# Transposes of q' in the rounded format, from buffers that DMAs fill, and rest products with 128 rows

## The chip, the cores and the metric

The kernel runs on one core of a Trainium2 chip. The metric is the device time of one execution, in microseconds (us); the median of several runs is given. The core's engines run beside each other: TensorE (PE; PEld are its weight loads), VectorE (DVE), ScalarE (ACT), GpSimd (POOL) and SyncE (SP). SP and POOL also issue the DMAs here.

## The reference

Two mixing blocks are gated together, with S = 2048 rows, D = 576 columns, H = 32 heads of Dh = 18:

```
g = sigmoid((x * gate_w).sum(-1, keepdims=True))
# a: linear attention
q, k, v = heads of x @ wqkv
pq, pk = phi(q), phi(k)          # phi(t) = (t + 1 if t > 0 else exp(t)) + 1e-6
kv = einsum("bhsd,bhse->bhde", pk, v);  z = pk.sum over s
o = (pq @ kv) / (pq @ z + 1e-6)
a = o @ wo
# b: real part of a 2-D DFT of a second input, by matrices
b = Cr @ (xb @ Dr.T) - Ci @ (xb @ Di.T)
out = g * a + (1 - g) * b
```

(In this kernel the second input is the same x.) All data are 32-bit floats.

## The kernel before, in words

**Products in a rounded format.** TensorE multiplies in fp32r (`R` in the code), a rounded 32-bit format. To keep precision, an operand is split in two: ScalarE writes its rounded value (`hi_of`, L196), VectorE writes the rest, `operand - hi` (`lo_of`, L206), and a product is made of three: hi·hi, hi·lo, lo·hi. Plain additions are `add` (L216). `run` (L226) issues a list of products into one of eight PSUM banks.

**The stages.** 576 columns are four chunks of 128 and a rest of 64; 2048 rows are 16 tiles of 128.

1. k' = phi(x wk) for all tiles (L558 and L226), to about 64 us, then the products of x with k' (L725) and with wv (L704, L707, the kv matrices in three PSUM banks), to about 134 us.
2. q' = phi(x wq) for 16 tiles, `q_tile` (L226, tiles `wd`, `xs`): 14 products for each half of 288 columns (290 in the second, which carries the gate). ScalarE (L393, L394) and VectorE (L395) turn each half into `acc[i]`. In between M = kv·wo is built (`build_kv`, `build_m`), moved by GpSimd's DMAs (`move_m`, L886 to L889) and split (`split_m`, tiles `mw`). `normalise(k)` divides the pair of tiles 2k, 2k+1 by the denominators, in four parts on VectorE (L796, L797, L800, L801, L804); for the transposes it copies the last 64 columns of both tiles to `last` (L809).
3. The attention's second product, `q' M`, from about 192 to 258 us, a loop over 16 tiles. `transposed(k)` turns a normalised pair on TensorE with the identity: eight transposes of 128x128 (L826) and one for the two rests (L827), in the full format, straight from `acc` into PSUM; ScalarE and VectorE split the result into `qs`. For each half of a tile 14 products with M follow (`m_steps`). ScalarE scales by the gate (L1239), and GpSimd stores the row to `att` (L1241). The pair k is turned in iteration 2k-1 (pair 0 at the end of stage 2).
4. `Hidden.run`, twice: the DFT along D for seven combinations of blocks (a Strassen-like scheme, `PRODUCTS`), 392 products at L1012. Each product of 576 is 6 products of 128 rows (tiles `xf` or `xb`) and one of 96 rows for the rest (tile `xr`; hi, lo and hi of 32 rows one below the other). `Left` and `right` prepare the combinations of x and of the DFT matrix, in pieces that run between other work: `right`'s third piece (k = 2) makes the rest rows.
5. `sequence`, after each `Hidden.run`: the DFT along S, 1344 products at L1171, whose matrices are combined and split by VectorE and ScalarE as they arrive, and the mixing with the gate (L1188).

**What sets the order.** SyncE, ScalarE and VectorE run in the order of the program's text (`manual_schedule`); ScalarE and VectorE from the first stage on. TensorE does so only from the loop of stage 3 on; before, the framework's scheduler orders it. GpSimd's queue is ordered by that scheduler all along. By hand are set: `early`, which says after which q' tile a part of `norms`, of the third piece or of x's pair 7 (`seven`) is done; `plan`, the same for stage 3; and the tables of iterations at which SyncE issues loads. `begin_after` makes an instruction wait for another one. All buffers lie at fixed addresses of one arena, and later uses of an address wait for earlier ones.

Of the kernel before, what the change touches and what calls it, by code (L numbers as in the profile page):

```python
# [142 lines left out]
def kernel(  # L143
# [111 lines left out]
    ident = const([P, P], F, "ident")  # L255
    make_identity(nc, ident)
# [142 lines left out]
    xrest = scratch([NP * 96, 7 * P], "xr")  # L399
    xrest_of = xrest.rearrange("(g q j r) n -> g j r q n", g=2, q=4, j=3)  # L400
# [54 lines left out]
    def right(src, rest, order):  # L455

        main, last = scratch([P, 7, 2, 2, HALF], "wm"), scratch([96, 7, HALF], "wm")

        def load(k, start):
            c = at(start, [P, 7, 2, HALF], R, "wb")[:P if k < 2 else 96]  # L460
            r, raw = c.bitcast(F)[:, :, 1], src[k] if k < 2 else rest
            for a, b in ((slice(0, 3), slice(0, 3)), (5, 3)):
                begin_after(nc.gpsimd.dma_start(out=r[:, a], in_=raw[:, b]), done[-1])
            return c

        def piece(k, start):

            c = load(k, start)
            r = c.bitcast(F)[:, :, 1]
            yield  # L470
# [4 lines left out]
            add(r[:, 6], r[:, 4], r[:, 1], ALU.subtract)  # L475
            yield
            hi_of(c[:, :, 0], r)
            yield
            if k < 2:
                for fs in (slice(0, 4), slice(4, 7)):  # L480
                    lo_of(c[:, fs, 1], r[:, fs], c[:, fs, 0])
                    nc.gpsimd.dma_start(out=main[:, fs, k], in_=c.bitcast(F)[:, fs])
                    if fs.start == 0:
                        yield
            else:
                rows = slice(32, 64)
                lo_of(c[rows, :, 0], r[rows], c[rows, :, 0])
                yield
                nc.gpsimd.dma_start(out=last, in_=c.bitcast(F)[:, :, 0])

        return (main, last), [piece(*o) for o in order]
# [127 lines left out]
    def xg_next(lo_of=lo_of):  # L619
        if xg_raw:  # L620
# [4 lines left out]
            else:  # L625
# [4 lines left out]
                                              (2, T_AT + 76544)))  # L630
# [145 lines left out]
    def q_tile(i):  # L776
# [14 lines left out]
    def normalise(k):  # L791
# [10 lines left out]
        for i in range(2):  # L802
# [4 lines left out]
            if i == 1:  # L807
                lasts.append(at(last_ring.next(), [P, 2, REST], F, "last"))
                nc.vector.tensor_copy(out=lasts[-1], in_=acc_pairs[k][:, :, KC * P:])  # L809
            yield  # L810

    lasts, last_ring = [], Ring(T_AT + 92672, 2 * REST * 4, 3)
# [5 lines left out]
    def transposed(k):  # L818

        both = [at(qs_ring.next(), [P, 9, P], R, "qs") for _ in range(2)]  # L820
        mains = [bank(), bank()]
        last = bank()[:, :P]
        for i in range(2):
            for c in range(KC):
                cs = slice(c * P, (c + 1) * P)
                nc.tensor.transpose(mains[i][:, cs], acc[2 * k + i][:, cs], ident)  # L826
        nc.tensor.transpose(last, lasts.pop(0).rearrange("p a b -> p (a b)"), ident)  # L827
# [3 lines left out]
        for i, t in enumerate(both):  # L831
            mine, other = ((slice(0, REST), slice(REST, P))[j] for j in (i, 1 - i))
            hi_of(t[mine, 8], last[mine])
            lo_of(t[other, 8], last[mine], t[mine, 8])
        return both
# [56 lines left out]
    def split_m(h):  # L892
        hi_of(mhi[:, :KC, h], mraw[:, :, h])
        lo_of(mlo[:, :, h], mraw[:, :, h], mhi[:, :KC, h])
        hi_of(mhi[:, KC, h], mrest[:, h])
# [15 lines left out]
    for f in wo_split:  # L911
        f()
    kv_step(4)
    q_tile(1)
    build_kv()
# [7 lines left out]
    early = {4: [(norms, 2)], 5: [(norms, 1), (wr_pieces[2], 1)],  # L923
             6: [(norms, 1)], 7: [(wr_pieces[2], 1)],
             8: [(wr_pieces[2], 1), (norms, 1)], 9: [(wr_pieces[2], 1), ("seven", 1)],
             10: [("seven", 1)], 11: [(wr_pieces[2], 1)],
             12: [(wr_pieces[2], 1), ("seven", 1)], 14: [("seven", 1), (norms, 1)],
             15: [("seven", 1), (norms, 1)]}
    for i in range(4, NT):
        for part in early.get(i, ()) if i > 12 else ():  # L930
            go(seven if part[0] == "seven" else part[0], part[1])
        q_tile(i)
# [5 lines left out]
        for part in early.get(i, ()) if i < 13 else ():  # L938
            go(seven if part[0] == "seven" else part[0], part[1])
        if i == NT - 3:  # L940
            queue = transposed(0)
        if i in (10, 11):
            split_m(i - 10)
# [26 lines left out]
    class Hidden:  # L970
# [4 lines left out]
        def load_w(self, k):  # L975
# [5 lines left out]
            nc.sync.dma_start(out=wl.bitcast(F), in_=self.main[:, f].rearrange("p c s n -> p (c s) n"))  # L981
            nc.sync.dma_start(out=rl.bitcast(F)[:96], in_=self.last[:, f])
            self.w[k] = wl, rl

        def load_rest(self, p):

            self.rest[p] = at(self.lay.rest(p), [P, 7, P], R, "xr")
            n = min(NP * 96 - p * 96, P)
            nc.sync.dma_start(out=self.rest[p].bitcast(F)[:n], in_=xrest[p * 96:p * 96 + n])

        def load_x(self, p, k):
# [3 lines left out]
            nc.sync.dma_start(out=t.bitcast(F), in_=xforms[p][:, a:b])  # L995
# [134 lines left out]
    def sequence(m, g, src, dst, last=None, between=None):  # L1130
# [100 lines left out]
    paced.enter_context(tc.manual_schedule(engines={mybir.EngineType.PE}))  # L1231
    for i in range(NT):
# [9 lines left out]
        go(norms, 1 if i in (4, 6) else 2)  # L1242
        for k, n in plan.get(i, ()):
            go(made[k], n)
# [150 lines left out]
```

## Time and profile before

| | |
|---|---|
| median of three runs | 716.61 us (716.57 to 717.23) |
| the profiled execution's own time | 717.38 us |
| its span, first to last instruction | 715.7 us |
| stage 3, from the first m_steps to the first L1012 | about 192.8 to 258.4 us |
| `Hidden.run`, first and second | 51.5 and 52.1 us |
| `sequence`, first and second | 175.2 us each on TensorE |

The page lists busy times, the groups of instructions by line and tile, the chain of work that ended last, and the DMAs. In a group's row stand the line, the engine, the operation, output<-inputs with moving operand first, the shape, the count; then busy time in us and the mean duration of one in ns; then the engine's idle time just before them. In the chain's rows stand start, length and what ran, in us. Durations of matmuls overlap, since they are pipelined: a product that lasts 293 ns holds TensorE for about 130 ns of the chain. A row of a timeline has start and length in us, and a row of the windows has the stretch, its length, and each engine's busy time. A row of DMAs has the count, the size, and the median time from issue to landing.

### The profile page before, as it was taken

Reading aid. Unit: us, or ns where it says so; the run is one execution under the profiler, and the core shown is the slowest. Engines: PE = TensorE matmul, PEld = TensorE weight load, DVE = VectorE, ACT = ScalarE, POOL = GpSimd, SP = SyncE. Lnnn points to the kernel's source line nnn. Section 1 sums busy time; section 2 is a strip of 40 time slices with the busy share of each in tenths; the row PEclk is TensorE's granted clock in tenths of the full one; section 3 lists DMA queues with packets and bytes.
Section 4 is the critical chain, followed back from the end, with each engine's and each line's share of the span. In section 5 each row is a group of like instructions: output and inputs, shape, how many; then the busy total and the mean of one; then the engine's idle time right before and its main releaser. Section 6 shows DMA issues by size and latency. Waiting matters only on the chain.

```text
span 715.7 us, 13965 instructions
## 1 busy us (share of the span) xinstructions
PE 711.6 (99%) x5436; PEld 711.1 (99%) x5436; DVE 601.1 (84%) x1020; ACT 338.5 (47%) x587; POOL 54.9 (8%) x94
## 2 busy tenths in 40 slices
PE   9999999999999999999999999999999999999998
PEld 9999999999999999999999999999999999999998
DVE  5699977687999748989999999857889988888885
ACT  5998445677644444553534334323535433343331
POOL 1112200050131110000010000000000000000000
PEclk9999999999999999999999999999999999999999
DMA  7388896874594589753475675789973544454530
GB/s 259 105 280 312 318 303 209 301 213 129 180 368 183 195 307 366 237 184 118 150 257 184 212 254 208 278 312 402 377 260 94 184 132 144 127 181 155 179 131 34
DMA packets 57525, 157.84 MB, mean 221 GB/s; under 512 B 6388, under 2 KB 15668, under 8 KB 56436
## 3 DMA queue, kind: packets, MB, share of 16 engines
q1 hardware_dynamic: 48404, 118.44, 48.9%
q0 software_dynamic: 8768, 38.12, 14.7%
q8 instruction: 43, 0.70, 0.4%
q10 hardware_dynamic: 288, 0.39, 0.2%
q14 instruction: 22, 0.18, 0.1%
HBM read 114.06 MB, written 41.39 MB: 217 GB/s over the span
## 4 chain that ended last, share of the span: by engine, by line
PE 99%; DVE 0%; issue 0%
PE bank L1171 49%; PE bank L226 23%; PE bank L1012 14%; PE bank L725 8%; PE bank L558 2%; PE bank L826 1%; PE bank L252 1%; PE bank L704 0%; PE bank L707 0%; PE bank L827 0%; DVE row L1188 0%
## 5 line engine op out<-in xcount | busy, mean ns | idle before, releaser
L1171 PE MATMUL bank<-fh,c 128*128 128x288 f32 x1792 | 350.7, 293 | 0.0
L1171 PEld LDWEIGHTS bank<-fh,c 128*128 128x128 f32 x1792 | 285.1, 188 | 0.0
L1171 PE MATMUL bank<-fl,c 128*128 128x288 f32 x896 | 262.3, 293 | 0.0
L196 ACT ACTIVATE c<-craw 128x768 fp32r<-128x768 f32 (+2 forms) x148 | 126.9, 900 | 163.6 <-DVE craw L216 154.0
L1171 PEld LDWEIGHTS bank<-fl,c 128*128 128x128 f32 x896 | 168.2, 188 | 0.0
L206 DVE TENSOR_TENSOR c<-craw,c 128x768 fp32r<-128x768 f32 (+3 forms) x148 | 146.1, 1024 | 0.8 <-ACT c L196 0.8
L226 PE MATMUL bank<-wd,xs 128*128 128x288 f32 (+1 forms) x784 | 104.9, 294 | 0.0
L226 PEld LDWEIGHTS bank<-wd,xs 128*128 128x128 f32 x784 | 103.5, 188 | 0.0
L1012 PE MATMUL bank<-wf,xf 128*128 128x288 f32 x588 | 90.8, 294 | 0.0
L1012 PEld LDWEIGHTS bank<-wf,xf 128*128 128x128 f32 x588 | 83.3, 189 | 0.0
L226 PE MATMUL bank<-mw,qs 128*128 128x288 f32 x448 | 60.7, 295 | 0.0
L725 PE MATMUL bank<-pk,c 128*128 128x288 f32 x448 | 60.0, 294 | 0.0
L725 PEld LDWEIGHTS bank<-pk,c 128*128 128x128 f32 x448 | 59.1, 188 | 0.0
L226 PEld LDWEIGHTS bank<-mw,qs 128*128 128x128 f32 x448 | 59.0, 188 | 0.0
L216 DVE TENSOR_TENSOR craw<-craw,craw 128x256 f32<-128x256 f32 x128 | 54.4, 425 | 5.1
L216 DVE TENSOR_TENSOR ys<-bank,ys 128x288 f32<-128x288 f32 x63 | 28.8, 457 | 28.2 <-PE bank L1171 25.7
L216 DVE TENSOR_TENSOR craw<-craw 128x512 f32<-128x512 f32 x64 | 43.9, 687 | 7.6 <-PE bank L1171 3.7
L196 ACT ACTIVATE fh<-fl 128x864 fp32r<-128x864 f32 (+1 forms) x36 | 30.3, 868 | 28.0 <-DVE fl L216 20.0
L395 DVE SCALAR_TENSOR_TENSOR acc<-bank,e 128x288 f32<-128x288 f32 x64 | 28.6, 454 | 16.5 <-ACT e L394 16.3
L206 DVE TENSOR_TENSOR fl<-fl,fh 128x864 fp32r<-128x864 f32 (+1 forms) x36 | 35.4, 988 | 1.6
L1012 PE MATMUL bank<-wf,xr 96*128 96x288 f32 x112 | 33.3, 298 | 0.0
L216 DVE TENSOR_TENSOR fl<-bank,y 128x288 f32<-128x288 f32 x48 | 21.8, 454 | 11.1 <-PE bank L1012 9.6
(106 smaller groups left out, 662.1 us busy)
## 6 DMA issues: line engine op xcount, KB each, us to landing
xf<-xm SPq DMA_DIRECT2D x42, 512.0 KB, 9.2
craw<-in_cr_dram SPq DMA_DIRECT2D x32, 512.0 KB, 3.9
craw<-in_ci_dram SPq DMA_DIRECT2D x32, 512.0 KB, 3.7
xm<-xb POOLq DMA_DIRECT2D x8, 1024.0 KB, 6.6
wf<-wm SPq DMA_DIRECT2D x14, 576.0 KB, 6.4
xraw<-in_xa_dram SPq DMA_DIRECT2D x25, 320.0 KB, 3.5
xr<-xr SPq DMA_DIRECT2D x14, 448.0 KB, 8.5
xm<-xb POOLq DMA_DIRECT2D x8, 768.0 KB, 8.2
```

The lines of the kernel that those rows point to most:

```text
L196: return nc.scalar.activation(dst, src, AF.Copy, bias=bias)
L206: nc.vector.tensor_tensor(out=dst, in0=src, in1=hi, op=ALU.subtract)
L216: nc.vector.tensor_tensor(out=dst, in0=a, in1=b, op=op)
L226: nc.tensor.matmul(ps, a, b, start=(n == 0), stop=(n == len(pairs) - 1))
L252: nc.tensor.matmul(warm[:, :136], unit[:, :P], unit, start=True, stop=True)
L395: nc.vector.scalar_tensor_tensor(dst, ps, 0.0, e, op0=ALU.max, op1=ALU.add)
L558: nc.tensor.matmul(ps[i][h], x[:, i_x * P:(i_x + 1) * P], wkt.row(h, j), start=(c == 0 and n == 0), stop=(c == KC and n == 1))
L725: nc.tensor.matmul(ps[h][:, :HALF], t[:, a, k], pk[s][:, b, half(h)], start=(s == 0 and n == 0), stop=(s == NT - 1 and n == len(turn) - 1))
L826: nc.tensor.transpose(mains[i][:, cs], acc[2 * k + i][:, cs], ident)
L1012: nc.tensor.matmul(ps, a, b, start=(start and n == 0), stop=(n == len(ops) - 1), skip_group_check=True)
L1171: nc.tensor.matmul(ps[q], c[x][l > 2][:, l - 3 * (l > 2), k], factors[p](y, f), start=(p == 0 and i == 0), stop=(p == NP - 1 and i == 2))
```

## The change

- The identity is made in the full format, then rounded by ScalarE into an `R` tile. `transposed` becomes a generator `turn`, whose 9 transposes have `R` input, identity and output.
- VectorE's copy to `last` goes. When a pair is normalised it is put on a list; `move_normal`, called at the end of each q' tile and of each iteration of stage 3, has GpSimd issue two DMAs for it: 4 x 128 columns of both tiles, and the 64 left of both, into buffers (`turn_at`) of type `R`. The transposes read these.
- TensorE runs in the text's order from `build_kv()` on. In `q_tile` the halves are mixed: 9 products of half 0, 9 of half 1, 5 of half 0, 5 of half 1. The transposes of pair 0 stand in the middle of q' tile 13.
- `split_m` becomes `m_hi` (after q' tiles 9 and 10) and `m_lo` (10 and 11).
- `early` and `plan` are rearranged; two more parts of `norms` are done before stage 3, and the parts of pairs 4 to 7 come one iteration earlier.
- The rest products of `Hidden` take 128 rows: the fourth 32 rows of the weights are zeros, the rows of x are whatever follows. The rest piece (`rest_piece`) works on 64 partitions with half the columns each, and stores eight blocks of 32 rows; x's rest tensor gets 32 rows of zeros at its end.
- The loads of x's pair 2 are spread over iterations 4, 6, 8 and 10, and these and the weights' loads wait for the ScalarE instruction that came last (`begin_after`). Near the end of the first `sequence` one rest load is issued later.

The diff, cut to its core:

```diff
-    ident = const([P, P], F, "ident")
-    make_identity(nc, ident)
+    unit_f = at(SLOT_AT + P * 4, [P, P], F, "unit_f")
+    make_identity(nc, unit_f)
+    ident = const([P, P], R, "ident")
+    nc.scalar.activation(ident, unit_f, AF.Copy)
...
+        def rest_piece(start):
+            c = at(start, [2 * 32, 3, 7, HALF // 2], R, "wb")
+            f = c.bitcast(F)
+            r = f[:, 1]
+            load(r, rest)
+            nc.gpsimd.memset(f[:, 2], 0.0)
+            yield
+            for _ in sums(r):
+                pass
+            yield
+            hi_of(c[:, 0], r)
+            yield
+            lo_of(c[:, 1], r, c[:, 0])
+            for k, a in enumerate((0, 1, 0, 2)):
+                for q in range(2):
+                    ps, cs = slice(q * 32, q * 32 + 32), slice(q * HALF // 2, (q + 1) * HALF // 2)
+                    nc.gpsimd.dma_start(out=last[k * 32:k * 32 + 32, :, cs], in_=f[ps, a])
+            if src is wr:
+                nc.gpsimd.dma_start(out=xrest[NP * 96:], in_=f[:32, 2].rearrange(
+                    "p f n -> p (f n)")[:, :7 * P])
...
-        for h in range(2):
-            ps = bank()[:, :QH[h]]
-            run(ps, steps(xs, lambda j: wqt.row(h, j)))
+        both = [bank()[:, :QH[h]] for h in range(2)]
+        todo = [list(steps(xs, lambda j, h=h: wqt.row(h, j))) for h in range(2)]
+        for part in (slice(0, 9), slice(9, 14)):
+            for h in range(2):
+                for n in range(part.start, part.stop):
+                    nc.tensor.matmul(both[h], *todo[h][n], start=(n == 0), stop=(n == 13))
+            if part.start == 0:
+                next(between, None)
...
-                lasts.append(at(last_ring.next(), [P, 2, REST], F, "last"))
-                nc.vector.tensor_copy(out=lasts[-1], in_=acc_pairs[k][:, :, KC * P:])
+                normal.append(k)
...
+    def move_normal():
+        while normal:
+            k = normal.pop(0)
+            main = at(turn_at[k], [P, 2, KC * P], R, "turn")
+            last = at(turn_at[k] + 2 * KC * P * 4, [P, 2, REST], R, "turn")
+            for t, cs in ((main, slice(0, KC * P)), (last, slice(KC * P, D))):
+                nc.gpsimd.dma_start(out=t.bitcast(F), in_=acc_pairs[k][:, :, cs])
+            moved.append((main, last))
...
-                nc.tensor.transpose(mains[i][:, cs], acc[2 * k + i][:, cs], ident)
-        nc.tensor.transpose(last, lasts.pop(0).rearrange("p a b -> p (a b)"), ident)
+                nc.tensor.transpose(mains[i][:, cs].bitcast(R), main[:, i, cs], ident)
+        nc.tensor.transpose(last.bitcast(R), rest.rearrange("p a b -> p (a b)"), ident)
+        yield
...
+    paced.enter_context(tc.manual_schedule(engines={mybir.EngineType.PE}))
     build_kv()
...
-    early = {4: [(norms, 2)], 5: [(norms, 1), (wr_pieces[2], 1)],
-             6: [(norms, 1)], 7: [(wr_pieces[2], 1)],
-             8: [(wr_pieces[2], 1), (norms, 1)], 9: [(wr_pieces[2], 1), ("seven", 1)],
-             10: [("seven", 1)], 11: [(wr_pieces[2], 1)],
-             12: [(wr_pieces[2], 1), ("seven", 1)], 14: [("seven", 1), (norms, 1)],
-             15: [("seven", 1), (norms, 1)]}
+    early = {4: [(norms, 2), (wr_pieces[2], 1)], 5: [(norms, 1)],
+             6: [(norms, 2), (wr_pieces[2], 1)], 7: [(wr_pieces[2], 1), (norms, 1)],
+             8: [(wr_pieces[2], 1), (norms, 1)], 9: [("seven", 1), (norms, 1)],
+             10: [("seven", 1), (norms, 1)], 12: [("seven", 1)], 14: [("seven", 1)],
+             15: [("seven", 1)]}
...
-            nc.sync.dma_start(out=rl.bitcast(F)[:96], in_=self.last[:, f])
+            if after is not None:
+                begin_after(move, after)
+            nc.sync.dma_start(out=rl.bitcast(F), in_=self.last[:, f])
...
-            ops.append((self.rest[p][:96, 6 - k], wl[:96]))
+            ops.append((self.rest[p][:, 6 - k], wl))
...
-        3: [(0, 1)], 4: [(0, 1)], 5: [(0, 1)], 6: [(0, 1)], 7: [(0, 1)],
-        11: [(1, 1)], 12: [(1, 1)], 13: [(1, 1)], 14: [(1, 2)],
+        2: [(0, 1)], 3: [(0, 1)], 5: [(0, 1)], 10: [(0, 1)], 11: [(0, 1), (1, 1)],
+        12: [(1, 1)], 13: [(1, 1)], 14: [(1, 2)],
...
-        go(norms, 1 if i in (4, 6) else 2)
+        go(norms, 1 if i in (3, 5) else 2)
         for k, n in plan.get(i, ()):
             go(made[k], n)
+        move_normal()
...
-        for k, j in enumerate((9, 10, 12, 4, 5, 6, 14)):
+        for k, j in enumerate((9, 10, 12, 3, 5, 7, 14)):
             if i == j:
-                hidden.load_w(k)
+                hidden.load_w(k, done[-1])
...
-        if i == 3:
-            hidden.load_pair(2)
+        for k, j in ((0, 4), (2, 6), (4, 8), (6, 10)):
+            if i == j:
+                hidden.load_x(2, k, done[-1])
```

More of the change, by code (lines that the diff above doesn't have):

```diff
@@ L475, in piece @@
             add(r[:, 6], r[:, 4], r[:, 1], ALU.subtract)
+        def piece(k, start):
+            c = at(start, [P, 7, 2, HALF], R, "wb")
+            r = c.bitcast(F)[:, :, 1]
+            load(r, src[k])
+            yield
+            yield from sums(r)
             yield
@@ L834, in transposed @@
             lo_of(t[other, 8], last[mine], t[mine, 8])
+    def transposed(k):
+        both = []
+        for _ in turn(k, both):
+            pass
         return both
@@ L931 @@
             go(seven if part[0] == "seven" else part[0], part[1])
-        q_tile(i)
+        if i == NT - 3:
+            queue = []
+            turning = turn(0, queue)
+            q_tile(i, turning)
+        else:
+            q_tile(i)
         build_m({4: (2, 3), 5: (4,)}.get(i, ()))
```

81 lines of the change are left out of this document (40 added, 41 removed).

## The prediction

> **What bounds the kernel now.** I read the page's busy shares and clock first, then the chain that ended last, then the groups by line and shape, and last the stretch from 134 to 258 us by windows and by timeline, since the diff edits little else.
>
> ```profile
> span 715.7 us, 13965 instructions
> PE 711.6 (99%) x5436; PEld 711.1 (99%) x5436; DVE 601.1 (84%) x1020; ACT 338.5 (47%) x587; POOL 54.9 (8%) x94
> PEclk9999999999999999999999999999999999999999
> PE 99%; DVE 0%; issue 0%
> ```
>
> TensorE is busy 711.6 of 715.7 us, at the full granted clock in every slice, and the chain that ended last is 99% TensorE. No wait is there to be removed. The time can fall only if some of the 5,436 matmuls become shorter, and it can rise if one of them has to wait. So I price each edit on TensorE, then ask which new wait could open a hole. The chain, in order of time, prices instructions in their place:
>
> ```profile
> 82.82 0.12 PE bank L704
> 82.94 0.06 PE bank L707
> 83.00 0.17 PE bank L704
> 83.17 0.06 PE bank L707
> ...
> 196.50 0.87 PE bank L826 x8
> 197.38 0.11 PE bank L827
> 197.49 7.29 PE bank L226 x56
> ...
> 258.40 51.52 PE bank L1012 x392
> 309.92 175.21 PE bank L1171 x1344
> 485.13 52.09 PE bank L1012 x392
> ```
>
> A pair of q' tiles costs 0.87 + 0.11 = 0.98 us for its nine transposes (L826, L827), that is 0.109 us each, and then 56 products with M. There are eight pairs, so all transposes hold TensorE for 7.8 us.
>
> **The transposes in the rounded format.** The count stays at 72, with data and identity in fp32r. No transpose of this kind is in the trace, so I look at neighbours.
>
> ```profile
> L826 PE MATMUL bank<-ident,acc 128*128 128x128 f32 x64 | 8.4, 272 | 0.0
> L826 PEld LDWEIGHTS bank<-ident,acc 128*128 128x128 f32 x64 | 7.5, 140 | 0.0
> L707 PE MATMUL bank<-gt,plain 128*126 128x126 f32 x20 | 4.4, 222 | 0.0
> L707 PE MATMUL bank<-gt,plain 128*72 128x72 f32 x5 | 1.0, 201 | 0.0
> L707 PEld LDWEIGHTS bank<-gt,plain 128*126 128x126 f32 x20 | 3.8, 189 | 0.0
> L707 PEld LDWEIGHTS bank<-gt,plain 128*72 128x72 f32 x5 | 0.7, 144 | 0.0
> ```
>
> L707 is a rounded matmul of 126 columns: 222 ns, and 0.06 us on the chain. From 72 to 126 columns the duration grows by 21 ns over 54 columns, 0.39 ns a column. The full-format transpose of 128 columns lasts 272 ns, 50 ns more than L707, which is just another 128 columns at 0.39 ns: its moving side looks like two passes, and a rounded one should need one. That gives 0.06 us a transpose.
>
> The weight load could spoil this. L704 after L707 costs 0.17 us instead of 0.12: a short matmul leaves the next load 0.05 us uncovered, and a pair of loads takes 0.17 + 0.06 = 0.23 us, 0.115 each. But transposes load in 140 ns, as long as an ordinary load of 72 columns, against 189 ns for 126. So a transpose's load looks short already, and I assume that this is a property of transposing and stays. The sum per pair: 9 x 0.06 + 0.05 for the first product after them, whose ordinary load is then uncovered, = 0.59 us against 0.98. That is 0.39 us less, times 8 = **3.1 us gained**. The bounds are 3.6 us (no uncovered load: 9 x 0.05 x 8) and -0.4 us (each held to 0.115: 9 x 0.115 = 1.035, 0.05 more per pair). I take 3.1, as the 140 ns row is the nearest.
>
> The Trainium skill speaks against it: by "TensorE: Matmul & The Clock Gate", section "LDWEIGHTS (loading the stationary operand)", a load takes its columns divided by 1.2 GHz, and its table of weight-path modes gives 32-bit formats no fast load. My estimate from that is 107 ns for any 128 columns, so transposes would stay at 0.107 us and gain nothing. The trace agrees for L707's pairs (0.115) but not for the transposes' 140 ns.
>
> **Rest products with 128 rows.**
>
> ```profile
> L1012 PE MATMUL bank<-wf,xf 128*128 128x288 f32 x588 | 90.8, 294 | 0.0
> L1012 PE MATMUL bank<-wf,xr 96*128 96x288 f32 x112 | 33.3, 298 | 0.0
> ```
>
> The 96-row products last 298 ns and their 128-row neighbours 294: 112 x 4 ns = **0.45 us gained**. Above, it can't exceed what the stage loses against L1171: 51.52/392 = 131.4 ns a product (132.9 in the second stage) against 175.21/1344 = 130.4, so 0.4 + 1.0 = 1.4 us. Below it is nothing, if the 4 ns belong to closing a group and not to the rows. The same section of the Trainium skill says that a load's time doesn't depend on rows; by that alone this term is nothing. The weights' added quarter is zeros.
>
> **TensorE in the text's order, halves mixed 9-9-5-5, high parts of M first.** The same 28 matmuls run per q' tile.
>
> ```profile
> 134.52 48.59 PE bank L226 x366
> ```
> ```profile
> L394 ACT ACTIVATE e<-e 128x288 f32<-128x288 f32 x64 | 28.5, 445 | 2.0
> L393 ACT ACTIVATE e<-bank 128x288 f32<-128x288 f32 x64 | 25.6, 399 | 11.2 <-PE bank L226 7.6 <-PE bank L558 3.6
> ```
> ```profile
> 158.96 0.59 POOL L889 DMA_DIRECT2D mw<-mf  x1 [1.32 <-issue]
> ```
> ```profile
> 175.11 1.48 ACT L196 ACTIVATE mw<-mw 128x1152 fp32r<-128x1152 f32 x2
> ```
>
> The chain has no hole here that a better order could close; at most the 48.59/366 = 132.8 ns a product would fall to the 130.4 of L1171, 0.9 us. A loss comes if an evacuation is late, now that the two halves of a tile end close together: 0.40 + 0.45 = 0.85 us of ScalarE, once. I cost it at nothing, as two banks per tile are held and eight exist. M's first half is split one tile (28 x 0.133 = 3.7 us) earlier than at 175.1, at 171.4; its last move was issued at 159.0, 12 us ahead.
>
> **The copies to the turn buffers.** This is the new wait. After normalising a pair, GpSimd issues two DMAs (512 and 64 KB), and the transposes of that pair wait for them; behind the waiting transposes stand all of TensorE's later matmuls. The copy of columns on VectorE (L809) goes.
>
> ```profile
> 242.33 1.43 DVE L804 SCALAR_TENSOR_TENSOR acc<-acc,den 128x576 f32<-128x576 f32 x2
> 243.79 0.23 DVE L809 COPY last<-acc 128x128 f32<-128x128 f32 x1
> ```
> ```profile
> 238.08 0.87 PE bank L826 x8
> 238.95 0.11 PE bank L827
> 239.06 7.34 PE bank L226 x56
> 246.40 0.87 PE bank L826 x8
> ```
> ```profile
> att<-acc POOLq DMA_DIRECT2D x10, 288.0 KB, 3.4
> xm<-xb POOLq DMA_DIRECT2D x1, 1024.0 KB, 5.9
> ```
> ```profile
> L1241 POOL DMA_DIRECT2D att<-acc x16 | 8.8, 547 | 47.9 <-ACT acc L1239 47.8
> L888 POOL DMA_DIRECT2D mw<-mf x1 | 0.6, 612 | 0.0
> ```
>
> The last pair is the tightest. It is normalised by 243.8 and turned at 246.4: 2.6 us. The change puts two more parts of the normalising into the q' stage, so pairs 4 to 7 finish one tile earlier, in iterations 4, 6, 8 and 10 for use in 7, 9, 11 and 13. A pair with its transposes takes 246.40 - 238.08 = 8.32 us, a tile half of it, 4.2 us. The cover is 2.6 + 4.2 = 6.8 us, less some 0.4 because TensorE is faster: 6.4 us. The need is two issues of about 0.6 us and a landing of 3.4 to 5.9 us (576 KB lies between those sizes): 4.6 to 7.1, middle 5.8. So I cost the copies at **nothing**, with 0.6 us of cover left in the middle case and up to 0.7 us missing at each of four pairs in the worst one of this stretch.
>
> VectorE must keep pace with a faster TensorE as well:
>
> ```profile
> 226.00:234.40 8.40, 7.80 (x15) 1.00 0.62 249
> 234.40:242.70 8.30, 7.27 (x14) 1.00 0.58 182
> ```
>
> It works 7.3 to 7.8 us of each 8.3 us pair (second number). A pair would take 7.9 us; VectorE loses 0.23 us of L809 per pair and two parts of 0.75 to 1.5 us altogether to the q' stage, where the rest piece shrinks by about as much (half as many columns per instruction, 64 partitions). It just fits.
>
> **What is moved on the queues.** SyncE's weight loads and the loads of x's pair 2 now wait for a ScalarE instruction of their iteration. Queued behind them are only loads for the stage at 258.4; the latest, of iterations 14 and 15, stand where they stood, so nothing. GpSimd gets eight stores instead of one for each rest piece, a small memset and the store of zeros: with 0.6 us each some 6 us, in the q' stage, on an engine busy 8% of the span. What stands behind them are copies needed tiles later. The identity's rounding on ScalarE lies at the start, long before its use.
>
> **The sum.** The profiled run took 717.38 us, 1.7 us outside its span and 0.8 above the median of 716.61. 717.38 - 3.1 - 0.45 = 713.8 for such a run; the median falls by the same 3.6, to **713.0**. About 0.2%, 1.4 us, is what a measurement of this kernel can tell from no change.
>
> **The rivals.** *The transpose keeps its pace* (chance 0.20). Either the load holds it to 0.115 us or transposing takes two passes in both formats. For it: the ordinary loads' 0.115, and that a rounded transpose isn't in the trace; against it: the 140 ns. Time: between 716.61 + 0.4 - 0.45 = 716.6 and, with 0.109 kept, 716.2. No measurable change.
>
> *The copies come late* (0.14), the case on the other side. Place: the transposes of pairs 4 to 7. It decides when issue and landing exceed 6.4 us. A store of xm ahead of the copy on GpSimd's queue, which waits for VectorE, or a landing as at the end of the q' stage would do it:
>
> ```profile
> xm<-xb POOLq DMA_DIRECT2D x1, 1024.0 KB, 9.9
> ```
>
> With that landing, 1.2 + 9.9 - 6.4 = 4.7 us are missing at a pair. With half of it, 2.3 us, at four pairs: 9 us lost against 3.6 won, 722. It outweighs the gain from 0.9 us a pair, and shows as slower from 1.25. Against it: the change spreads the loads that fill the DMA queues in that time.
>
> *VectorE paces the pairs* (0.06): with 7.8 us and the 0.3 us that it waits for ScalarE in each pair, it allows 8.1 instead of 7.9, and half of the gain stays: 714.8.
>
> **How the numbers follow.** Forecast 0.60, rivals 0.20, 0.14, 0.06. Faster by over 0.2% (below 715.2): 0.60 + 0.06 less a little for small stalls, 0.64. Same: 0.20 + 0.02 = 0.22. Slower: 0.14. The low end takes half of what the three upper bounds lie above the values taken (0.5 transposes, 0.95 rest, 0.9 order): 713.0 - 1.2 = 711.8. The high end takes in the first rival with 0.115 (716.6) and half of the order's loss and of its missing rest term: 717.2. The forecast's own range is 711.8 to 714.8.
>
> **What would show it.** Right: L826 at about 222 ns and 0.06 us on the chain, the first product after them about 0.05 longer, pairs every 7.9 us, L1012's rest group at 294 ns, no idle on TensorE. Wrong: transposes still at 0.11 us on the chain with equal durations (first rival), or idle before L826 put down to DMA turn (second), or to VectorE before L226 (third).

## The result, and the profile after

The changed kernel takes 723.67 us (median of six runs, 721.50 to 724.95); the kernel before, on the same chip, 717.14 us (716.57 to 717.75). The ratio is 1.0087, with an interval of 1.0075 to 1.0099: slower by 6.5 us, where 3.6 us of gain were forecast. The profiled execution took 722.13 us, 1.5 below its median, and its span grew by 4.7 us; so the profile shows somewhat less than the whole loss.

The page of the kernel after: span, busy time, share of the chain that ended last.

```profile
span 720.4 us, 14032 instructions
PE 711.4 (99%) x5436; PEld 710.6 (99%) x5436; DVE 595.4 (83%) x1012; ACT 336.4 (47%) x588; POOL 76.7 (11%) x127
PE 93%; DMA 3%; issue 2%; POOL 1%; DVE 0%; ACT 0%; POOLq 0%; SPq 0%
```

TensorE's busy time hardly changed, yet the span is 4.7 us longer, and the chain, 99% TensorE before, now has links through DMAs and GpSimd. Its waits, by line, in us in total, number, longest:

```profile
PE bank L1069 <- DMA wf<-wm: 2.4, 1, 2.4
PE bank L863 <- DMA turn<-acc: 1.8, 1, 1.8
...
PE bank L864 <- DMA turn<-acc: 0.7, 1, 0.7
```

L863 and L864 are the transposes, which wait for the new copies; L1069 is the product of the hidden stage (L1012 before), which waits for its weights: it is the seventh product of x pair 0. What the change was priced to shorten, on the chain and in the groups:

```profile
196.16 0.64 PE bank L863 x8
196.80 0.09 PE bank L864
196.89 7.42 PE bank L226 x56
204.31 0.64 PE bank L863 x8
204.95 0.08 PE bank L864
205.03 7.37 PE bank L226 x56
212.41 0.02 issue
```
```profile
L863 PE MATMUL bank<-ident,turn 128*128 128x128 f32 x64 | 6.5, 245 | 1.8 <-DMA turn<-acc 1.8
...
L863 PEld LDWEIGHTS bank<-ident,turn 128*128 128x128 f32 x64 | 6.2, 140 | 2.0 <-DMA turn<-acc 2.0
...
L1069 PE MATMUL bank<-wf,xr 128*128 128x288 f32 x112 | 33.2, 297 | 0.0
```
```profile
490.24 51.72 PE bank L1069 x392
```

A pair's nine transposes take 0.73 us in place of 0.98. A pair with its 56 products takes (212.41 - 196.16)/2 = 8.12 us in place of 8.32, 1.6 us over eight pairs. The second hidden stage takes 51.72 in place of 52.09 us. Both gains are there. (The mean of 297 ns for the rest products takes in some that ran at half the clock, see below.) What eats them is on the chain of waits, in order of time:

```profile
222.08 8.31 DMA turn<-acc
230.39 0.04 issue
230.43 0.87 PE bank L863 x8
...
253.14 3.49 DMA att<-acc
...
256.77 10.60 DMA wf<-wm
267.37 0.14 issue
267.51 47.52 PE bank L1069 x350
```

The copy of pair 5 lands 8.31 us after its issue, and TensorE starts at once when it is there: the copy was what it waited for. The last weights need 10.60 us, after they have waited for a store of the attention rows (`att`), whose buffer they take. The last two loads of weights issue at 255.07 and 256.77 us, close together; in the kernel before they issue at 246.73 and 254.50. Windows of the span show why: stretch, length, busy time of PE, PEld, DVE, ACT, POOL, granted clock, share of the DMA engines, GB/s. First the kernel before, then after:

```profile
217.00:221.00 4.00, 4.00 (x33) 4.00 (x31) 3.88 (x7) 3.07 (x5) 0.56 (x1) 1.00 0.19 74
221.00:231.00 10.00, 10.00 (x82) 10.00 (x81) 9.16 (x16) 4.66 (x11) 1.92 (x4) 1.00 0.65 236
...
241.00:254.00 13.00, 13.00 (x103) 13.00 (x102) 6.54 (x15) 6.86 (x14) 1.62 (x3) 1.00 0.59 191
```
```profile
217.00:221.00 4.00, 4.00 (x35) 4.00 (x35) 2.44 (x5) 3.01 (x6) 0.67 (x2) 1.00 0.97 312
221.00:231.00 10.00, 8.18 (x67) 7.95 (x65) 6.97 (x12) 3.47 (x9) 3.43 (x6) 1.00 1.02 358
...
241.00:254.00 13.00, 12.28 (x98) 12.16 (x97) 5.46 (x13) 5.93 (x13) 3.70 (x7) 1.00 0.97 360
```

In each of these stretches the DMA engines went from partly idle (0.19, 0.65, 0.59) to full. And the copies don't leave GpSimd when a pair is ready. From the timeline of GpSimd (start, length, line, what, idle before):

```profile
213.24 0.57 POOL L1297 DMA_DIRECT2D att<-acc  x1 [1.48 <-ACT acc L1295]
215.04 0.70 POOL L847 DMA_DIRECT2D turn<-acc  x1 [1.22 <-DVE qs L206]
216.37 0.72 POOL L847 DMA_DIRECT2D turn<-acc  x1 [0.63 <-issue]
...
221.38 0.57 POOL L1297 DMA_DIRECT2D att<-acc  x1 [3.00 <-ACT acc L1295]
222.08 1.45 POOL L847 DMA_DIRECT2D turn<-acc  x2
```

| pair | normalised | first copy issued | copies landed | transposes waited |
|---|---|---|---|---|
| 4 | 210.68 | 215.04 | 220.03, 220.43 | no |
| 5 | 219.54 | 222.08 | 230.39, 230.60 | 1.82 us |
| 6 | 229.14 | 230.72 | 237.48, 237.65 | no |
| 7 | 239.18 | 240.49 | 245.42, 248.12 | 0.72 us |

Each first copy issues 1.3 to 4.4 us after its pair is ready: it stands behind the `att` store of the iteration, which waits for ScalarE. Ahead of the copies of pairs 4 and 6 GpSimd then stands idle for another 1.2 and 0.6 us; the last section comes back to that.

After the longest idle time TensorE runs at half its clock. The third-last column is the granted clock:

```profile
267.51:271.14 3.63, 3.63 (x16) 3.63 (x17) 1.64 (x3) 0.10 (x1) 0.00 (x0) 0.53 1.03 421
```

The sixteen products from 267.51 take 3.7 us; at 0.131 each they would take 2.1, so 1.6 us are lost. The account of the span: -1.6 (transposes), +1.8 and +0.7 (pairs 5 and 7), +0.2 (the transposes behind the wait, 0.87 in place of 0.64), which is +1.1; then the first hidden stage, which starts 1.2 us later than before (259.47 against 258.24) and ends 5.1 us later (315.03 against 309.92): +3.9, which is +2.4 for the wait for weights and +1.6 for the clock, less some 0.1 gained; and -0.4 in the second hidden stage. That is +4.6 of the 4.7 us.

### The profile page after: what moved, and what is told of

The parts are those of the page before. It is cut to its first block, busy times and chain, and to the rows that moved or that the text cites. A ratio compares the mean times of both kernels' runs of the same rounds, so it can differ in the third digit from the quotient of the medians.

```text
span 720.4 us, 14032 instructions
## 1 busy us (share of the span) xinstructions
PE 711.4 (99%) x5436; PEld 710.6 (99%) x5436; DVE 595.4 (83%) x1012; ACT 336.4 (47%) x588; POOL 76.7 (11%) x127
## 4 chain that ended last, share of the span: by engine, by line
PE 93%; DMA 3%; issue 2%; POOL 1%; DVE 0%; ACT 0%; POOLq 0%; SPq 0%
PE bank L1228 49%; PE bank L1069 14%; PE bank L226 10%; PE bank L803 8%; PE bank L745 8%; PE bank L578 2%; DMA wf<-wm 1%; DMA turn<-acc 1%; PE bank L252 1%; DMA att<-acc 0%; PE bank L724 0%; DVE qs L206 0%; PE bank L863 0%; POOL att L1297 0%; ACT qs L196 0%
## 5 line engine op out<-in xcount | busy, mean ns | idle before, releaser
L1069 PE MATMUL bank<-wf,xf 128*128 128x288 f32 x588 | 90.2, 294 | 0.0
L1069 PEld LDWEIGHTS bank<-wf,xf 128*128 128x128 f32 x588 | 82.7, 188 | 0.1
L803 PE MATMUL bank<-wd,xs 128*128 128x288 f32 (+1 forms) x448 | 60.8, 296 | 0.0
L226 PE MATMUL bank<-wd,xs 128*128 128x288 f32 x336 | 44.2, 293 | 0.0
```

The lines of the kernel that those rows point to most:

```text
L226: nc.tensor.matmul(ps, a, b, start=(n == 0), stop=(n == len(pairs) - 1))
L803: nc.tensor.matmul(both[h], *todo[h][n], start=(n == 0), stop=(n == 13))
L1069: nc.tensor.matmul(ps, a, b, start=(start and n == 0), stop=(n == len(ops) - 1), skip_group_check=True)
```

## The experiments

My theory after this profile: both gaining parts gain, less than forecast; the loss has two sources, copies that come late from GpSimd, and last weights that come late because `plan` puts two stores of the left operand (`xm`, for x pair 0) 19 and 13 us later, to 241.95 and 243.98 us, where 222.97 and 231.23 stood before. (The expectations call these stores those of x pair 7, and the product that waits for the weights that of x pair 2; by the kernel's text both belong to x pair 0.) Rivals: the reordering of q' or VectorE's order costs it; or only DMA bandwidth counts, and neither queue nor place does.

### The gaining parts alone

`turn_only` is the kernel before with the rounded transposes only. VectorE writes the normalised pair in the rounded format itself, so the low part of q' is left out of the transposed operand, here and in each build below without copies.

```diff
-    ident = const([P, P], F, "ident")
+    ident = const([P, P], R, "ident")
...
-            nc.vector.scalar_tensor_tensor(a, a, EPS,
+            to = acc_r[k][:, i].rearrange("p (h d) -> p h d", d=DH)
+            nc.vector.scalar_tensor_tensor(to, a, EPS,
...
-                nc.tensor.transpose(mains[i][:, cs], acc[2 * k + i][:, cs], ident)
+                nc.tensor.transpose(mains[i][:, cs].bitcast(R), acc_r[k][:, i, cs], ident)
```

> The kernel before, with the transposes alone changed: identity, data and output in the rounded format, and no copies by DMA. For this VectorE writes the normalised pair in the rounded format, so the low part of q' that the transposes carried is left out. Theory (a rounded transpose is held by its weight load, 0.085 us, and leaves the next product's load uncovered): 0.17 us less per pair, 1.4 us in all, 715.8. The prediction's own pace of 0.06 us: 3.1 us, 714.0. Rival (the pace in the changed kernel came from somewhere else, such as the buffers): no change, 717.1.

It took 716.07 us against 717.26, ratio 0.998 (0.9972 to 0.9989). Its chain:

```profile
203.93 0.64 PE bank L830 x8
204.57 0.08 PE bank L831
204.65 7.42 PE bank L226 x56
212.07 0.63 PE bank L830 x8
```

0.08 us a transpose, as in the kernel after, with no copy and no reordering in the way. So 0.06 us was the wrong size; the gain is 1.2 us by medians, 1.6 by the chain. The time stands near the 715.8 of the theory, not the 714.0 of the prediction's pace.

`rest_only` is the kernel before with the 128-row rest products and their rest piece alone (`ops.append((self.rest[p][:, 6 - k], wl))` in place of `[:96]`).

> The kernel before, with the rest products alone changed to 128 rows, their stores and loads with them. Theory (a product of 96 rows costs some 3 to 4 ns more): 0.35 us less in each of the two stages, 0.7 us in all, 716.4. Rival (the wider loads and the eight small stores per rest piece delay something): at or above 717.1, with a wait of TensorE in the first stage of the DFT along D.

716.74 us against 717.26, ratio 0.9996 (0.9987 to 1.0005).

```profile
L1029 PE MATMUL bank<-wf,xr 128*128 128x288 f32 x112 | 33.0, 294 | 0.0
258.25 51.46 PE bank L1029 x392
484.91 51.72 PE bank L1029 x392
```

The rest products last 294 ns in place of 298. The first hidden stage gains 0.06 us (51.46 against 51.52), the second 0.37 (51.72 against 52.09): 0.43 together, not the 0.35 in each that I expected. A gain of that size is in the chain; the time alone can't tell it from nothing.

`turn_rest` puts both into the kernel before.

> The kernel before with two parts of the change alone: transposes in the rounded format, which VectorE writes itself (q's low part in the transposed operand is left out), and the rest products on 128 rows. No copies, no new place for stores and loads, no text order in q'. Theory A (these two parts are the whole gain, and they add up): 717.1 - 1.2 - 0.5 = 715.4 us. Theory B (with both, TensorE reaches the last weights earlier than they land): a wait of 0.3 to 1 us ahead of the products of x pair 2, 716 us.

714.82 us against 717.17, ratio 0.9968 (0.9958 to 0.9979), with no wait of TensorE in this stretch. It beats both kernels, with the low part of q' left out.

### The copies

`nocopy` is the changed kernel without copies, `nocopy2` the same, built without the first one's fault.

```diff
-            for t, cs in ((main, slice(0, KC * P)), (last, slice(KC * P, D))):
-                nc.gpsimd.dma_start(out=t.bitcast(F), in_=acc_pairs[k][:, :, cs])
-            moved.append((main, last))
+            nc.vector.tensor_copy(out=last, in_=acc_r[k][:, :, KC * P:].bitcast(F))
+            moved.append((acc_r[k][:, :, :KC * P], last))
```

> The changed kernel without the copies to the turn buffers: the transposes read the pair where VectorE wrote it. VectorE writes it in the rounded format, so the low part of q' is left out. Theory (TensorE waits for copies that come late): no idle before the transposes; 717.1 - 1.4 - 0.7 = 715.0 if the last weight load of the first DFT stage is then on time as well, 718.6 if that stays late by itself. Rival (the order of TensorE in the q' stage, or the rearranged normalising, costs the time): 721 or more.

726.55 us, ratio 1.013 (1.0116 to 1.0144), and one wait:

```profile
PE bank L866 <- DMA xf<-xm: 9.3, 1, 9.3
```

This time says nothing for or against the theory: I had put the small `last` buffers where x pair 2 is loaded, so pair 7's last transpose waited for that load and read what it had written; the build doesn't compute the kernel's function. Up to there no transpose waited.

> Leaves out q's low part in the transposed operand: VectorE writes the normalised pair in the rounded format itself, and the transposes read it from there; the 64 last rows go to the buffers that the changed kernel has for them. All else is the changed kernel. Theory A (the copies and what they collide with cause the late pairs): no transpose waits for a DMA, the gaps of 1.8 and 0.7 us go, pairs cost 0.80 us each; if the weights of the product of x pair 2 also come on time, 723.7 - 1.8 - 0.9 - 2.4 - 1.2 = about 717; if the last weights are still late because the stores of the left operand lie late, the 2.4 us wait stays and it is 720 to 721. Theory B (the pairs are late for another reason, such as VectorE's order of work): gaps of over 0.5 us stay ahead of pairs 5 and 7, and the time stays at 722 to 724.

718.98 us, ratio 1.0033 (1.0020 to 1.0046). One wait in the stretch:

```profile
PE bank L1070 <- DMA wf<-wm: 2.0, 1, 2.0
```

No transpose waits, so the copies made the gaps at pairs 5 and 7, not VectorE's order. The weights are still late, without any copy: a second cause. The time lies between the two that theory A gave, nearer to that for late weights. (The profiled execution took 717.60 us, 1.4 below the median.)

`sp_copies` keeps the copies and has SyncE issue them.

```diff
-                nc.gpsimd.dma_start(out=t.bitcast(F), in_=acc_pairs[k][:, :, cs])
+                nc.sync.dma_start(out=t.bitcast(F), in_=acc_pairs[k][:, :, cs])
```

> The same 16 copies, issued by SyncE in place of GpSimd. Theory A (on GpSimd's queue the copies stand 1.3 to 4.4 us behind stores, partly because a queue with about 1024 descriptors outstanding takes no more): a copy issues within 0.7 us of the end of its normalising, unless SyncE is waiting for the spread loads; with landings of 4 to 8 us the gaps ahead of pairs 5 and 7 shrink from 1.8 and 0.7 us to under 0.5 each; the last weights stay late, so 720 to 722. Theory B (only DMA bandwidth matters, not the queue): the gaps and 723 to 724 stay. Theory C (SyncE's queue is blocked by the loads that wait for done products): copies are later than before, gaps grow, 725 or more.

719.69 us, ratio 1.0029 (1.0020 to 1.0038), 4.0 us less than the changed kernel by medians. Its only wait here:

```profile
PE bank L1069 <- DMA wf<-wm: 2.2, 1, 2.2
```

Pair 5 is normalised at 219.09, its first copy issued at 219.12 and landed at 224.70, 3.3 us before its transposes: 5.6 us from issue to landing in place of 8.3. The same bytes on the same DMA engines are on time when they aren't queued behind `att`. Theories B and C fall. The edit moves the copies to another queue and to an earlier time at once; what each is worth, this run doesn't tell.

### The place of the loads

`early_loads` takes the waits (`begin_after`) off the loads, with the copies on GpSimd.

```diff
-                hidden.load_w(k, done[-1])
+                hidden.load_w(k)
...
-                hidden.load_x(2, k, done[-1])
+                hidden.load_x(2, k)
```

> The changed kernel, but the loads of x's pair 2 and of the weights in the loop of q' M do not wait for ScalarE, so that they are issued as early as their buffers allow, as before. The copies stay on GpSimd's queue. Theory, first half (copies land late because the loads run at the same time): landings fall from 5 to 8 us to 3 to 5, TensorE no longer waits at the transposes, about 717 to 719. Second half (copies are issued late because they stand behind the store of att on GpSimd's queue): issue stays 1.3 to 4.4 us after the pair is normalised, and some wait stays. Rival (loads are not it): landings and waits as before, 722 to 724.

725.40 us, ratio 1.0112 (1.0098 to 1.0125).

```profile
PE bank L863 <- DMA turn<-acc: 4.7, 2, 3.0
PE bank L1069 <- DMA wf<-wm: 2.2, 2, 1.3
```

Three x loads and two loads of weights now issue from 205 to 210 us and meet the copy of pair 4, which issues 5.65 us after its pair is ready and lands at 223.37, 7.02 us later. The collision moved, and the waits grew; none of the three forecasts held. Spreading the loads is no mistake of the change where GpSimd copies. Nor is this the place that they have in the kernel before: there the loads of x pair 2 and the first weights issue at 188 to 193 us. By the kernel's text the buffers of the first three pairs' copies lie where x pair 2 is loaded, and the first of these loads issues at 205.07, as the transposes of pair 2 end. So these buffers already move the loads by some 17 us. (`nocopy_early` below keeps part of them, and its loads start at 205.71.)

### The place of the stores

`plan` is the changed kernel with the two late parts of x pair 0 made earlier.

```diff
-        2: [(0, 1)], 3: [(0, 1)], 5: [(0, 1)], 10: [(0, 1)], 11: [(0, 1), (1, 1)],
+        2: [(0, 1)], 3: [(0, 1)], 5: [(0, 1)], 6: [(0, 1)], 7: [(0, 1)], 11: [(1, 1)],
```

> The changed kernel, with the parts of the left operand for x pair 7 made in iterations 2, 3, 5, 6, 7 of the first stage after q' instead of 2, 3, 5, 10, 11, so its stores come some 20 us earlier (near 223 to 231 us, as in the kernel before). Theory A (the late weights come from these stores, which fill the DMA engines from 241 to 254 us): the last weights land before 265 us, the 2.4 us wait and the half clock behind it (1.2 us) go: 720 us; the stores then meet the copies of pairs 5 and 6, whose gap grows by up to 2 us: 720 to 722. Theory B (the late weights come from the copies and the attention stores alone): the wait stays above 2 us and the time at 723 to 724.

721.87 us, ratio 1.0059 (1.0044 to 1.0074).

```profile
PE bank L863 <- DMA turn<-acc: 3.5, 2, 2.2
PE bank L1069 <- DMA wf<-wm: 0.5, 1, 0.5
```

The wait for weights shrinks from 2.4 to 0.5 us, and the copies of pairs 5 and 6 pay: theory A, collision included. The profiled execution took 719.24 us, 2.6 below the median, so these rows show less than the whole loss.

`sp_plan` makes both edits, `nocopy_plan` has the earlier stores and no copies.

> Both edits: copies issued by SyncE, the stores of the left operand some 20 us earlier. Theory A (both the queue of GpSimd and the place of the stores matter): neither gap ahead of the transposes over 0.5 us nor a wait for weights over 0.5 us: 716 to 718, which is the kernel before less 1.4 (transposes) and 0.7 (rest products) plus what is left of the gaps. Theory B (the DMA engines simply have 8 x 1.2 MB too much to move in 217 to 268 us): one of the waits is left, 720 to 723.

717.56 us, ratio 1.0008 (0.9997 to 1.0019).

```profile
PE bank L863 <- DMA turn<-acc: 1.5, 2, 1.2
```

The time is that of theory A and the wait for weights is gone, but 1.2 us are left at pair 6, more than it allowed.

> The changed kernel without the copies (VectorE writes the pair in the rounded format, q's low part in the transposed operand is left out) and with the stores of the left operand some 20 us earlier. Theory A (copies and place of the stores are the whole loss): no wait of over 0.5 us on TensorE, 715.3 us, as with the two gaining parts in the kernel before. Theory B (the spread loads or the text's order in q' cost something of their own): 716.5 us or more with no wait that the copies or the stores explain.

715.41 us, ratio 0.9974 (0.9964 to 0.9984), no wait in the stretch. So with copies and late stores gone, the rest of the change (text order in q', halves, spread loads, M's high parts) costs some 0.6 us, by which `turn_rest` is lower; the two intervals overlap, so it may be nothing.

The same edit turned round, in the kernel before, is `before_late`: the parts of iterations 6 and 7 go to 10 and 11.

```diff
-        3: [(0, 1)], 4: [(0, 1)], 5: [(0, 1)], 6: [(0, 1)], 7: [(0, 1)],
-        11: [(1, 1)], 12: [(1, 1)], 13: [(1, 1)], 14: [(1, 2)],
+        3: [(0, 1)], 4: [(0, 1)], 5: [(0, 1)], 10: [(0, 1)], 11: [(0, 1), (1, 1)],
+        12: [(1, 1)], 13: [(1, 1)], 14: [(1, 2)],
```

> The kernel before, with one edit: the last two parts of the left operand for x pair 7 in iterations 10 and 11 in place of 6 and 7, as the changed kernel has them. Theory A (the place of these stores alone makes the last weights late): TensorE waits 1.5 to 3 us for the weights of the product of x pair 2, with some half-clock products behind it: 719 to 721 us. Theory B (late weights need the copies or the spread loads as well): a wait under 0.5 us, 717 us.

717.40 us, ratio 0.9999 (0.9991 to 1.0008), and no wait. My theory A fell in this form. By the trace's packets the last weights landed at 263.51 us, needed at 264.36; in the kernel before 258.87, needed at 263.76. The late stores take 4.0 of the 4.9 us of margin and stop there. Something else must take the rest, so two more runs: the late stores with TensorE's shorter stage (`turn_rest_late`, the same edit in `turn_rest`), and `nocopy2` with the loads not held back (`nocopy_early`, the edit of `early_loads`).

> The kernel before with the rounded transposes and the 128-row rest products (q's low part in the transposed operand is left out), and the last two parts of the left operand for x pair 7 in iterations 10 and 11 in place of 6 and 7. Theory A (the late stores take 4 us of the last weights' margin of 4.5 to 4.9 us, and nothing is lost until something else takes the rest): a wait under 0.5 us, 714.8 to 715.5 us. Theory B (the stores together with a TensorE that is 2 us earlier are enough): a wait of 1 to 2.5 us, 716.5 to 718.5 us.

715.29 us, ratio 0.9988 (0.9966 to 1.0010), no wait in the profile, as in theory A: the last weights land at 258.74, 3.0 us before their need (4.5 us before it in `turn_rest`). But two of its ten runs took over 720 us.

> The changed kernel without the copies (as in the second build without them: VectorE writes the pair in the rounded format, q's low part in the transposed operand is left out), with the loads for the hidden products at the places of the kernel before in time: none of them waits for a product's end. The stores of the left operand stay late. Theory A (what the late stores do not explain of the 2.0 us wait comes from the spread loads, which put an x load and two weight loads into 239 to 250 us): the wait falls under 0.7 us, 715.5 to 716.5 us. Theory B (stores late on TensorE's shorter time are enough, the spread loads do nothing): the wait stays at 1.5 to 2.5 us, 718 to 719.5 us.

717.11 us, ratio 1.0000 (0.9985 to 1.0016), no wait in the profile, against 2.0 us in `nocopy2`: the weights land 0.46 us before their need. The wait falls as in theory A; the time lies between the ranges of the two theories. Its ten runs lie between 714.94 and 721.22 us. So the spread loads take what margin the stores leave; that with so little left a run can go either way is my guess. Which wait the long runs had, here and in `turn_rest_late`, no trace shows.

### The whole change with its DMAs rearranged

`sp_early` is `sp_copies` with the loads not held back, `sp_plan_early` the same with the earlier stores.

> The copies issued by SyncE and the loads for the hidden products not held back by a product's end (as in the build with early loads); the stores of the left operand stay late. Nothing is left out. Theory A (the spread loads are what is late beside the stores): the 2.2 us wait for weights of the build with SyncE's copies falls under 0.7 us, and the copies of pair 4 land 1 to 3 us later than there but before their transposes: 715.5 to 717.5 us. Theory B (with the copies in the DMA queues, early loads only move the collision, as they did with GpSimd's copies): a wait of 1.5 us or more at pair 4 or 5 or at the weights, 718.5 to 721 us.

719.82 us, ratio 1.0032 (1.0020 to 1.0044), with 2.0 us of waiting for weights.

> Copies issued by SyncE, the stores of the left operand some 20 us earlier, and the loads not held back. Nothing is left out, so this is the whole change with only its queue and its order of DMAs as in the kernel before. Theory A (the gaps of 1.2 and 0.3 us ahead of pairs 6 and 7 with SyncE's copies and early stores come from the spread loads, which share the DMA engines with stores and copies): no gap over 0.5 us, 715 to 716.3 us, faster than the kernel before. Theory B (stores and copies alone collide): a gap of 1 us or more ahead of pair 6 stays, 716.5 to 718 us.

717.28 us, ratio 1.0006 (0.9996 to 1.0015), with 1.3 us at pair 6 and 0.7 us at the weights.

Both miss their theory A and lie in the range of theory B, but test less than I meant: SyncE works in the text's order, so the loads now stand behind the copies. The first one behind pair 4's copy issues at 211.96 us, where `early_loads` had them at 205 to 210. What the spreading costs beside copies stays open.

The medians in one line of steps (they come from several chips, on which the kernel before took 717.14 to 717.17 us):

| build | us |
|---|---|
| changed kernel | 723.67 |
| copies issued by SyncE (`sp_copies`) | 719.69 |
| no copies (`nocopy2`) | 718.98 |
| and the stores early (`nocopy_plan`) | 715.41 |
| the two gaining parts in the kernel before (`turn_rest`) | 714.82 |

## Why the prediction was wrong

The steps that turned a gain into a loss are two terms taken as nothing: the copies, and what is moved on the queues. A third, the transposes, was mis-sized.

**The transposes.** "That gives 0.06 us a transpose" was the first step to fail: 3.1 us forecast, 1.6 on the chain. In `turn_only`, pairs 1 to 7, the first two transposes of a pair last 222 to 230 ns, as the row of L707 had it, and the next one starts 57 to 67 ns behind each; those behind them last 244 to 254 ns, 79 to 91 apart. That fits a pace set by their loads; no run tells the load from the transposing itself. I had both bounds (0.05 and 0.115) and leaned on the 140 ns row, which is a duration and no cadence: it is the same 140 ns for the full-format transposes at 0.109 and for the rounded ones at 0.08. The rule that I set against the change, 107 ns a load by "TensorE: Matmul & The Clock Gate", section "LDWEIGHTS (loading the stationary operand)" of the Trainium skill, doesn't hold for the rounded transposes either: most start 79 to 91 ns apart. Another section of that page of the Trainium skill, "Back-to-back issue gap", states some 81 ns for a pair of load and matmul of 128 columns; the 0.08 us here agrees with that.

**Rest products.** 0.45 forecast for both stages; 0.43 on the chain of `rest_only`, 0.53 on that of `turn_rest`, and the row fell from 298 to 294 ns, as said. Right in size and sign. But the gain isn't 4 ns on each of 112 products: 0.37 of it lies in the second stage, 0.06 to 0.16 in the first, and no run shows why.

**The text's order in q'.** Taken as nothing, and nothing that can be told apart: it is one part of the 0.6 us above.

**The copies at nothing.** This step failed in its need, not in its cover. The cover was larger than 6.4 us: pair 5 was normalised 9.1 us before its transposes were due (219.54, 228.6). But the need held no time for the queue, and a landing of at most 5.9 us, from a stretch whose DMA engines were partly idle. In place of that the first copies waited 1.3 to 4.4 us and landed in 4.9 to 8.3. The rival "the copies come late" had the place right. Of its two conditions the long landing came true; a store ahead of the copy came too, but one of `att`, not of `xm`. `sp_copies` shows the copies' place on GpSimd's queue to be worth 4.0 us.

**"What is moved on the queues ... so nothing."** No rival held this step. I went through SyncE's loads and the rest piece's stores, and passed over `plan`, which moves two stores of 1 and 0.75 MB on GpSimd's queue, and what stands behind them in the DMA engines: the stores of `att`, whose buffers the last weights take. I took "loads for the stage at 258.4" as free because that stage lies later, without asking how long before their need they land: 4.9 us in the kernel before. The stores' place is worth 1.8 us with the copies on GpSimd's queue (`plan`), 2.1 with them on SyncE's (`sp_plan`) and 3.6 without copies (`nocopy2` to `nocopy_plan`); `before_late` shows that it costs nothing where the margin is whole.

**What "Against it" said** of the copies, that the spread loads make room for them, did not hold for 217 to 231 us, where the share rose to 0.97 and 1.02: there the spread loads and the copies meet. But loads that weren't held back met the copy of pair 4 (`early_loads`).

## What to carry to other kernels

When a change adds or moves DMAs, write down for each transfer already there when it is issued, landed and needed, and let every moved store take from that margin, also on transfers that the diff doesn't name: a margin of 5 us was used up here by two edits, later stores and spread loads. Alone, the later stores cost nothing in the kernel before (`before_late`), and the spread loads were part of 0.6 us at most by medians (`nocopy_plan`). A copy that must come promptly doesn't belong behind a store that waits for another engine. The pace of short matmuls is read from the chain, as length over count for the same kind of operand, and not from one instruction's duration.

## What the runs showed of the hardware

**Half clock after a short idle time.** TensorE's clock fell to half about the end of idle times of 2.4 us (`after`), 2.2 (`sp_copies`), 2.0 (`sp_early`) and 3.0 (`early_loads`), and stayed there for 3.4 us each time (267.73 to 271.14, 263.92 to 267.34, 264.92 to 268.33 and 223.37 to 226.78). In `sp_early` it fell only 0.9 us after TensorE had started again, at 264.00:

```profile
264.92:268.33 3.41, 3.41 (x16) 3.41 (x15) 1.97 (x3) 0.41 (x1) 0.00 (x0) 0.50 1.02 413
```

In `nocopy2` it did not fall after 2.0 us (1.00 granted from 265.01 to 267.00 us), nor in `plan` after 2.2 us (1.00 from 239.97 to 242.00), so idle time alone doesn't tell where it begins.

**GpSimd seems to hold a DMA back while too many rows are on the way.** The second copy of pair 4 issued at 216.37, 0.31 us after a load landed (216.06), the first one at 215.04, 0.34 us after a store did (214.70). The profile puts the wait of the first one down to VectorE's `qs`; but in `sp_copies` the same copy left 0.07 us after its pair was normalised, so it needs no `qs`. Count 128 rows for a store and 256 for a load of x or a copy, as the kernel's text has them. From 190 to 270 us of `after`, `plan` and `early_loads`, no DMA of this queue issued that brought the rows under way over 896. Of seventeen that would have reached 1,024 or more, fifteen issued 0.31 to 0.34 us after the landing that made room, and two later, right behind another DMA of the queue. The count fits all of them; it was not tested apart from the order of the queue.

**A pair of 0.98 us of transposes in the full format is 0.73 in the rounded one**, with the same 140 ns load records in both.
